# Attention and two expert layers on one core: dividing by the softmax row sums after the product with the values instead of before it

## The chip, the cores and the metric

The kernel runs on 1 core of one Trainium2 chip. The metric is the device time of one execution in microseconds (us), the median of several executions. The engines are named as in the profile: PE (TensorE matmul), PEld (TensorE weight load), DVE (VectorE), ACT (ScalarE), POOL (GpSimd) and SP (SyncE, which here issues every DMA).

## The reference

```python
scores = scale * np.matmul(q, k.transpose(0, 1, 3, 2))
...
scores = np.where(causal, -1000000000.0, scores + np.minimum(bias, 0.0))
scores = scores - np.max(scores, axis=-1, keepdims=True)
attn = np.exp(scores)
attn = attn / (np.sum(attn, axis=-1, keepdims=True) + 1e-09)
return np.matmul(attn, v).astype(np.float32)
...
x = np.ascontiguousarray(attn_out.transpose(0, 2, 1, 3)).reshape(B * S, H * D)
a = x @ w_a
b = x @ w_b
return (a * b @ w_out).astype(np.float32)
...
h = x @ w_in
r = np.maximum(h, 0.0)
g = r * r
return (g @ w_out).astype(np.float32)
```

There are 4 batches of 8 heads, 576 positions and a head dimension of 64; `bias` comes from a running sum of `s`. The attention's output, 2304 tokens of 512 numbers, goes through a gated layer (512 to 1536 and back) and then through a second layer (512 to 2048 and back). Everything is 32-bit.

## The kernel before

**Order of the work.** One function records all operations into a `Plan` (L73 to L246) and the plan then decides, by a table of costs and by ranks (L77), on which of its allowed engines each operation runs and in what order each engine's queue stands. An operation may list several engines: `on_dve`, `on_act`, `on_gps` (L324 to L330). Each queue is then executed in that fixed order. All engine instructions are issued at L246, so the profile's rows all say L246 and are told apart by tile names. Every DMA is issued by SP, in one queue.

**Stages.** Attention of batch 0 is recorded first (stream "first", L936). Then come the twelve steps of the first token chunk of the gated layer, each with the decoding of its weights (`split_w`, L805: rearranging 64-bit words into 32-bit numbers, on DVE, ACT and POOL), and in between, the attention of batch 1 (stream "next"). The attention of batches 2 and 3 is recorded beside further chunks of the gated layer (L950 to L953), and the rest of that layer and the second layer follow. A chunk of the gated layer needs the attention output of its tokens from all four pairs of heads: the first chunk needs 512 positions of batch 0.

**Attention of one head.** `softmax` (L554) makes scores in four PSUM banks (tiles `st`, L461), adds the mask and takes the row maximum on DVE (`neg`), and lets ACT write the exponentials into `e` and their row sums into `sum`. Then one DVE reduction adds the partial sums of all five blocks of queries, one DVE instruction takes the reciprocal (both `one`, L626 and L630), and the five blocks of `e`, 64 to 576 columns wide, 1600 columns in all, are multiplied by it in place, each on DVE, ACT or POOL as the plan likes (L631 to L642). `weigh` (L645) transposes pieces of `e` on PE (`pt`), copies them to SBUF (`ph`), and multiplies them with the values (`av`); its transposes read the "w" parts of `e`, which the multiplications write. The result, 64 rows a head, is copied to `u` (two heads of a pair fill its 128 partitions). In batches 2 and 3 the operands are split in a high and a low part, and `u` is the sum of two halves of `av`.

**Where `u` goes.** `attention` (L711) rounds `u` of batch 0 to a high and a low part (`x0`, both read by the first chunk's matmuls `ab`) and writes its last 64 columns to DRAM (`xd`); for the other batches all of `u` goes to `xd`, from where later chunks load it.

Of the kernel before, what the change touches and what calls it, by code (L numbers as in the profile page):

```python
# [7 lines left out]
F32 = mybir.dt.float32  # L8
# [8 lines left out]
P = 128  # L17
# [231 lines left out]
def attention_moe_moe(tc, q, k, v, s, w_a, w_b, w_out, w_in2, w_out2, out):  # L249
# [55 lines left out]
    def scratch(shape, dtype, name):  # L305
        return pl.fixed(lambda: pools["dram"].tile(shape, dtype, name=name))
# [63 lines left out]
    wlo = [scratch([HD, P, 2, GRP, P], F32, f"wlo{g}") for g in range(NG)]  # L370
    cd = scratch([B * H, 2, S], F32, "cd")


# [76 lines left out]
    for i in range(4):  # L450
        t = [at_const([P, *n], F32, f"{z}{i}") for z, n in (("neg", [NJ + 2]), ("sum", [NJ, 3]), ("one", [NJ]))]
        for x in t[::2]:
            gps("memset", NJ + 2, x, 1.0)

        for c, x in ((0, 1.0), (1, 0.0), (2, 1e-9)):
            gps("memset", NJ, t[1][:, :, c : c + 1], x)
        small.append(t)
# [95 lines left out]

    def softmax(b, p, h, head):  # L554

        nq = len(kb)
        nm = f"{b}_{p}_{h}"
        hh = 2 * p + h
        neg, tot, one = small[count[1] % 4]
        count[1] += 1  # L560
        place = {}
        held = []
        for i, pieces in enumerate(banks):
# [60 lines left out]
            held = []  # L624
        qs = slice(0, nq)
        dve(  # L626
            "tensor_reduce", 3 * nq, out=one[:, qs], in_=tot[:, qs], op=ALU.add, axis=AX.X,
            reads=[tot.part(c) for c in range(nq + 1)],
        )
        dve("reciprocal", nq * 6, one[:, qs], one[:, qs])  # L630
        for blk, (e, off) in place.items():  # L631
            at_, m = kb[blk]
            n = at_ + m
            ee, r = e[:m, off : off + n], one[:m, blk : blk + 1]
            parts = [(blk, 0)] if n <= 512 else [(blk, 0), (blk, 288)]
            kw = {"reads": [e.part(x) for x in parts]}
            ways = [on_dve("tensor_scalar", n, ee.part((blk, "w")), ee, r, None, op0=ALU.mult, each=0.52)]
            ways.append(on_act("mul", n, ee.part((blk, "w")), ee, r))
            ways.append(
                on_gps("tensor_tensor", n, out=ee.part((blk, "w")), in0=ee, in1=r.to_broadcast([m, n]), op=ALU.mult)  # L640
            )
            pl.call(*ways)  # L642
        return place

    def weigh(b, p, h, head, place, chunk, u):  # L645
# [4 lines left out]
        for i, keys in enumerate(key_banks):  # L650
            ps = bank(f"pt{nm}_{i}", "t")
            calls, ins, off, spans = [], [ident], 0, []
            for j in keys:
                k0, m = kb[j]
                c0 = max(k0, g0)
                for blk in range(j, len(kb)):
                    at_, mq = kb[blk]
                    if g0 <= at_ < g0 + n:
                        e, eo = place[blk]
                        ins.append(e.part((blk, "w")))  # L660
                        col = off + at_ - c0
                        calls.append(
                            ("transpose", (ps[:m, col : col + mq], e[:mq, eo + k0 : eo + k0 + m], ident[:mq, :mq]), {})
                        )
                w = g0 + n - c0
                spans.append((j, m, c0 - g0, w, off))
                off += w
# [36 lines left out]


    first = [[at([P, FIRST], F32R, "x0", 2 * ND, f"x0{z}_{d}") for d in range(ND)] for z in range(2)]

# [3 lines left out]
    def attention(b):  # L711
        steps = []

        def unit(p):
# [5 lines left out]
            def one(h):  # L720
                def f():
                    if h == 0:
                        st["u"] = at([P, S], F32, "u", 1, f"u{b}_{p}")
                    place = softmax(b, p, h, st["h"][h])
                    for chunk in weight_banks:
                        weigh(b, p, h, st["h"][h], place, chunk, st["u"])
                    if h == 1:
                        u = st["u"]
                        if b == 0:
                            xh, xl = first_x(p, 0, FIRST)  # L730
# [464 lines left out]
```

## Time and profile before

| | |
|---|---|
| median of 3 runs | 1093.37 us (1091.91 to 1094.2) |
| profiled execution, its own time | 1088.79 us |
| its span, first to last instruction | 1087.0 us |
| PE busy | 1054.8 us (97%), 5376 matmuls |
| PEld busy | 920.4 us (85%) |
| DVE busy | 707.7 us (65%) |
| ACT busy | 502.2 us (46%) |
| POOL busy | 307.6 us (28%) |

The profile is of one execution. An engine's busy time is the union of its instructions; matmuls overlap in it, so a busy PE need not be at its peak. The row of PE in 40 slices of the span reads `5998999999999999999999999999999999999998` and that of DVE `5877899988877888736747445676546434652432`: the first quarter of the span and the rest differ.

### The profile page before, as it was taken

The page shows a single profiled execution, that of the slowest core. Times are in us where ns is not written, and L with a number is a line of the kernel's source. Part 1 is how long each engine was busy: PE and PEld are TensorE (multiplying, and loading weights), DVE is VectorE, ACT ScalarE, POOL GpSimd, SP SyncE. Part 2 cuts the span into 40 slices and gives each one's busy share as a digit, 9 for nine tenths or more (in the row PEclk, how much of TensorE's full clock was granted, in tenths as well). Part 3 has the DMA queues.
Part 4 walks back from the last instruction along what each step waited for, and adds up shares of the span by engine and source line. Part 5 has one row for each costly group of instructions (what it writes and reads, how often), then busy time and mean ns, then how long its engine had stood idle before and what let it go on. Part 6 is the DMA issues. An engine that isn't in the chain of part 4 may idle for free.

```text
span 1087.0 us, 15586 instructions
## 1 busy us (share of the span) xinstructions
PE 1054.8 (97%) x5376; PEld 920.4 (85%) x5376; DVE 707.7 (65%) x1494; ACT 502.2 (46%) x1169; POOL 307.6 (28%) x263
## 2 busy tenths in 40 slices
PE   5998999999999999999999999999999999999998
PEld 3655777777899998999999999998988899889887
DVE  5877899988877888736747445676546434652432
ACT  4665777666667556624333123354423222332222
POOL 2535657565333324105224202323202000200000
PEclk9988999999999999999999999999999999999999
DMA  6543576756544446248879777364535333343311
GB/s 201 173 131 114 177 216 211 230 167 191 160 151 141 141 136 191 85 134 287 293 253 313 258 265 250 142 253 172 192 144 187 146 123 136 112 163 122 136 69 58
DMA packets 94063, 190.84 MB, mean 176 GB/s; under 512 B 10256, under 2 KB 56336, under 8 KB 93984
## 3 DMA queue, kind: packets, MB, share of 16 engines
q1 hardware_dynamic: 93984, 189.85, 51.8%
q8 instruction: 42, 0.69, 0.3%
q14 instruction: 37, 0.30, 0.1%
HBM read 143.58 MB, written 37.37 MB: 166 GB/s over the span
## 4 chain that ended last, share of the span: by engine, by line
PE 86%; DVE 8%; DMA 3%; issue 1%; ACT 1%; SPq 1%; POOL 0%; ACTq 0%; DVEq 0%; POOLq 0%
PE ab L246 24%; PE po L246 18%; PE py L246 11%; PE pa L246 9%; PE av L246 6%; PE st L246 5%; PE pt L246 5%; PE pc L246 5%; PE pb L246 2%; DVE e L246 1%; DVE roomxl L246 1%; DVE st L246 1%; SPq L246 1%; DMA roomxl<-in_moe_w_out 1%; DMA raw_2q<-in_q 1%
## 5 line engine op out<-in xcount | busy, mean ns | idle before, releaser
L246 PE MATMUL ab<-x,wh 128*128 128x512 f32 (+1 forms) x384 | 117.0, 386 | 0.0
L246 ACT ACTIVATE e<-st,neg 128x192 f32<-128x192 f32 (+2 forms) x192 | 91.2, 479 | 38.4 <-DVE neg L246 33.5
L246 PE MATMUL ab<-xh,wh 128*128 128x448 f32 x288 | 106.2, 369 | 0.0
L246 PE MATMUL ab<-xl,wh 128*128 128x448 f32 x288 | 105.3, 366 | 0.0
L246 PE MATMUL ab<-xh,lo 128*128 128x448 f32 x288 | 105.2, 365 | 0.0
L246 ACT COPY s<-pa 128x384 f32<-128x384 f32 x72 | 34.4, 481 | 137.8 <-PE pa L246 137.7
L246 PE MATMUL pt<-ident,e 128*128 128x128 f32 (+2 forms) x480 | 83.8, 284 | 12.4 <-DVE e L246 7.7
L246 PE MATMUL py<-gh,wh 128*128 128x448 f32 (+1 forms) x240 | 90.7, 378 | 0.0
L246 PE MATMUL po<-w2o,gxh 128*128 128x512 f32 x288 | 89.3, 391 | 0.0
L246 PE MATMUL po<-w2o,gh 128*128 128x512 f32 x288 | 89.2, 391 | 0.0
L246 PE MATMUL py<-gh,loo 128*128 128x448 f32 (+1 forms) x240 | 89.0, 371 | 0.0
L246 PE MATMUL py<-gl,wh 128*128 128x448 f32 (+1 forms) x240 | 88.9, 371 | 0.0
L246 PEld LDWEIGHTS pt<-ident,e 128*128 128x128 f32 (+2 forms) x480 | 54.2, 135 | 37.8 <-issue 10.7
L246 DVE TENSOR_TENSOR ab<-ab,a 128x448 f32<-128x448 f32 (+1 forms) x60 | 38.6, 643 | 67.6 <-PE ab L246 64.0
L246 PEld LDWEIGHTS ab<-x,wh 128*128 128x128 f32 x384 | 71.7, 190 | 9.5
L246 PE MATMUL av<-ph,val 128*128 128x256 f32 (+3 forms) x256 | 78.3, 397 | 1.4 <-DVE u L246 0.7
L246 DVE CUSTOM_DVE_ANT_0 st<-st,mask 64x64 f32<-64x64 f32 (+4 forms) x160 | 68.2, 434 | 13.8 <-PE st L246 8.6
L246 ACT CAST gh<-ab 128x448 fp32r<-128x448 f32 (+1 forms) x60 | 32.6, 543 | 85.0 <-DVE ab L246 84.9
L246 DVE TENSOR_TENSOR v<-pc,s 128x384 f32<-128x384 f32 x48 | 26.6, 554 | 68.3 <-ACT s L246 67.2
L246 PEld LDWEIGHTS po<-w2o,gh 128*128 128x128 f32 x288 | 53.5, 188 | 9.2
L246 ACT COPY a<-ab 128x448 f32<-128x448 f32 (+1 forms) x60 | 32.5, 542 | 62.2 <-PE ab L246 61.8
L246 PEld LDWEIGHTS po<-w2o,gxh 128*128 128x128 f32 x288 | 53.4, 188 | 8.6
(247 smaller groups left out, 2733.5 us busy)
## 6 DMA issues: line engine op xcount, KB each, us to landing
w<-w2q SPq DMA_DIRECT2D x48, 896.0 KB
lo<-wlab SPq DMA_DIRECT2D x48, 512.0 KB
loo<-wlo SPq DMA_DIRECT2D x40, 384.0 KB
w2r<-in_moe_w_in SPq DMA_DIRECT2D x16, 512.0 KB
w2or<-in_moe_w_out SPq DMA_DIRECT2D x16, 512.0 KB
w2q<-w2h SPq DMA_DIRECT2D x8, 896.0 KB
w2q<-w2l SPq DMA_DIRECT2D x8, 896.0 KB
roomxh<-in_moe_w_a SPq DMA_DIRECT2D x10, 512.0 KB
```

The costliest lines, as they stand in the source:

```text
L246: getattr(eng, method)(*map(real, args), **{k: real(a) for k, a in kw.items()})
```

## The change

The multiplication of the 1600 columns of `e` by the reciprocal sums is gone, and the transposes read the exponentials as ACT leaves them. In its place the result `u` of a pair of heads, 576 columns, is multiplied. There the row sums belong to columns, so they have to be turned round and spread over 64 partitions each: in batch 0 by spreading them to 128 columns (`wide`, on ACT or DVE) and transposing five pieces on PE into PSUM (`rs`), from which DVE multiplies; in the other batches by one small transpose, a copy (`rows`), a DMA to DRAM (`rd`) and two DMAs that read it back once for each of 64 partitions (`wide`), after which POOL or DVE multiplies. `u` and the reciprocals get two buffers.

```diff
-    def softmax(b, p, h, head):
+    def softmax(b, p, h, head, one):
...
-        qs = slice(0, nq)
+        qs = one[:, h * nq : h * nq + nq].part(h)
         dve(
-            "tensor_reduce", 3 * nq, out=one[:, qs], in_=tot[:, qs], op=ALU.add, axis=AX.X,
+            "tensor_reduce", 3 * nq, out=qs, in_=tot[:, :nq], op=ALU.add, axis=AX.X,
             reads=[tot.part(c) for c in range(nq + 1)],
         )
-        dve("reciprocal", nq * 6, one[:, qs], one[:, qs])
-        for blk, (e, off) in place.items():
...
-            pl.call(*ways)
+        dve("reciprocal", nq * 6, qs, qs)
         return place
...
-                        ins.append(e.part((blk, "w")))
+                        ins += [e.part((blk, x)) for x in ((0,) if at_ + mq <= 512 else (0, 288))]
...
+    def divide_far(b, p, one, u):
+
+        nq = len(kb)
+        ps = bank(f"rs{b}_{p}", "t")
+        pe(107, [("transpose", (ps[: 2 * nq, :P], one, ident), {})], ps, [one.part(0), one.part(1), ident])
+        rows = at([P, P], F32, "rows", 2, f"rows{b}_{p}")[: 2 * nq]
+        copy(P, rows, ps[: 2 * nq, :P], psum=True)
+        far = rd[b, p]
+        dma(far, rows, 2)
+        wide = at([P, nq * P], F32, "wide", 2, f"wide{b}_{p}")
+        for h in range(2):
+            dma(
+                wide[h * D : h * D + D].part(h),
+                far[h * nq : h * nq + nq].rearrange("(o j) q -> o (j q)", o=1).to_broadcast([D, nq * P]), 164,
+            )
+        for o, n, w in ((0, 64, 0), (64, S - 64, P)):
+            kw = {"out": u[:, o : o + n].part("r"), "in0": u[:, o : o + n].part("r"), "in1": wide[:, w : w + n], "op": ALU.mult}
+            pl.call(
+                on_gps("tensor_tensor", n, **kw), on_dve("tensor_tensor", n, two=True, **kw),
+                reads=[u.part((a, g)) for a in (0, 64) for g, _, _ in weight_banks],
+            )
+
+    def divide(b, p, one, u):
+
+        nq = len(kb)
+        if b:
+            return divide_far(b, p, one, u)
+        wide = at([P, nq * P], F32, "wide", 2, f"wide{b}_{p}")
+        copy(
+            nq * P, wide.rearrange("p (j h d) -> p j h d", j=nq, h=2),
+            one.rearrange("p (h j o) -> p j h o", j=nq, o=1).to_broadcast([P, nq, 2, D]),
+        )
+        for g0, n, key_banks in weight_banks:
+            ps = bank(f"rs{b}_{p}_{g0}", "t")
+            calls = []
+            for j, (at_, m) in enumerate(kb):
+                if g0 <= at_ < g0 + n:
+                    r = wide[:m, j * P : j * P + P]
+                    calls.append(("transpose", (ps[:, at_ - g0 : at_ - g0 + m], r, ident[:m, :m]), {}))
+            pe(len(calls) * 107, calls, ps, [wide, ident])
+            dve(
+                "tensor_tensor", n, out=u[:, g0 : g0 + n].part((0, g0)), in0=u[:, g0 : g0 + n].part((0, g0)),
+                in1=ps[:, :n], op=ALU.mult, reads=[u.part((64, g0))],
+            )
...
-                        st["u"] = at([P, S], F32, "u", 1, f"u{b}_{p}")
-                    place = softmax(b, p, h, st["h"][h])
+                        st["u"] = at([P, S], F32, "u", 2, f"u{b}_{p}")
+                        st["one"] = at([P, 2 * len(kb)], F32, "one", 2, f"one{b}_{p}")
+                    place = softmax(b, p, h, st["h"][h], st["one"])
...
+                        divide(b, p, st["one"], u)
```

The plan makes a new order out of this. Three places of it follow; in the names the first digits are batch, pair and head, the last number only counts tiles.

**First head, PE.** Before, the first transposes `pt` of the exponentials of head 0 stand behind the last scores `st` of both heads:

```order
L246 MATMUL st0_0_1_1_171<-fk1_81,fq1_89 128x448
L246 MATMUL st0_0_1_1_171<-fk1_81,fq1_89 64x64
L246 MATMUL st0_0_0_2_178<-fk0_77,fq0_79 128x288
L246 MATMUL st0_0_1_2_185<-fk1_81,fq1_89 128x288
L246 MATMUL st0_0_0_3_190<-fk0_77,fq0_79 128x288
L246 MATMUL st0_0_1_3_200<-fk1_81,fq1_89 128x288
L246 MATMUL pt0_0_0_0_0_236<-ident_73,e0_0_0_1_176 64x64
L246 MATMUL pt0_0_0_0_0_236<-ident_73,e0_0_0_0_164 64x128 x2
L246 MATMUL pt0_0_0_0_1_241<-ident_73,e0_0_0_0_164 128x128 x3
```

Now:

```order
L246 MATMUL st0_0_1_1_163<-fk1_81,fq1_89 128x448
L246 MATMUL st0_0_1_1_163<-fk1_81,fq1_89 64x64
L246 MATMUL st0_0_0_2_170<-fk0_77,fq0_79 128x288
L246 MATMUL pt0_0_0_0_0_177<-ident_73,e0_0_0_1_168 64x64
L246 MATMUL pt0_0_0_0_0_177<-ident_73,e0_0_0_0_157 64x128 x2
L246 MATMUL pt0_0_0_0_1_181<-ident_73,e0_0_0_0_157 128x128 x3
L246 MATMUL st0_0_1_2_188<-fk1_81,fq1_89 128x288
L246 MATMUL st0_0_0_3_194<-fk0_77,fq0_79 128x288
L246 MATMUL av0_0_0_0_199<-ph0_0_0_0_0_186,val0_0_96 128x320
L246 MATMUL av0_0_0_0_199<-ph0_0_0_0_1_190,val0_0_96 128x256
L246 MATMUL st0_0_1_3_209<-fk1_81,fq1_89 128x288
```

The first two groups of transposes have moved ahead of three of the last score matmuls.

**End of batch 0, PE.** `ab` are the first matmuls of the gated layer. Before, scores and transposes of batch 1 stand ahead of the first of them:

```order
L246 MATMUL st1_0_1_0_1016<-t2k1_0_1_879,t2q1_0_1_871 128x320
L246 MATMUL st1_0_1_0_1016<-T11_912 128x192
L246 MATMUL st1_0_1_0_1016<-t2k1_0_1_879,t2q1_0_1_871 128x192
L246 MATMUL st1_0_1_1_1026<-T11_912 128x448
L246 MATMUL st1_0_1_1_1026<-t2k1_0_1_879,t2q1_0_1_871 128x448
L246 MATMUL st1_0_1_1_1026<-T11_912 64x64
L246 MATMUL st1_0_1_1_1026<-t2k1_0_1_879,t2q1_0_1_871 64x64
L246 MATMUL pt1_0_0_0_0_1049<-ident_73,e1_0_0_1_972 64x64
L246 MATMUL pt1_0_0_0_0_1049<-ident_73,e1_0_0_0_949 64x128 x2
L246 MATMUL pt1_0_0_0_1_1055<-ident_73,e1_0_0_0_949 128x128 x3
L246 MATMUL ab0_0_0_1063<-x00_0_424,wh0_0_273 128x512
L246 MATMUL ab0_0_0_1063<-x01_0_431,wh0_0_273 128x512
```

Now:

```order
L246 MATMUL av0_3_1_320_904<-ph0_3_1_320_0_891,val0_3_572 128x256 x2
L246 MATMUL rs0_3_0_909<-ident_73,wide0_3_867 128x64
L246 MATMUL rs0_3_0_909<-ident_73,wide0_3_867 128x128 x2
L246 MATMUL av0_3_1_320_904<-ph0_3_1_320_1_902,val0_3_572 128x256
L246 MATMUL rs0_3_320_921<-ident_73,wide0_3_867 128x128 x2
L246 MATMUL av0_3_1_320_904<-ph0_3_1_320_1_902,val0_3_572 128x128
L246 MATMUL av0_3_1_320_904<-ph0_3_1_320_2_913,val0_3_572 128x256
L246 MATMUL ab0_0_0_958<-x00_0_394,wh0_0_288 128x512
L246 MATMUL ab0_0_0_958<-x01_0_404,wh0_0_288 128x512
```

The transposes `rs` stand between the last products with the values, and `ab` follows directly on them; the 20 score matmuls and 6 transposes of batch 1 that stood ahead of the first `ab` come behind its group of 12.

**SP, a pair of batch 1.** Before, `u` goes to DRAM in one step, between loads of weights (`roomxh`, `roomxl`) and values:

```order
L246 DMA roomxl_152<-in_moe_w_out 128x1024
L246 DMA wlo1_1215<-wl4_2_1390 256x1x128 x2
L246 DMA val1_2_1435<-in_v 64x128
L246 DMA xd1_1448<-u1_0_1118 128x576
L246 DMA roomxh_130<-in_moe_w_b 128x4x256
L246 DMA val1_2_1435<-in_v 128x4x128
L246 DMA wlab5_1477<-wl5_1416 128x1024
```

Now, of the same pair:

```order
L246 DMA wlo1_1159<-wl4_2_1350 256x1x128 x2
L246 DMA rd1_0_1397<-rows1_0_1384 10x128
L246 DMA roomxh_129<-in_moe_w_b 128x4x256
L246 DMA wide1_0_1420<-rd1_0_1397 64x640 x2
L246 DMA val1_2_1448<-in_v 64x128
L246 DMA val1_2_1448<-in_v 128x4x128
```

The small `rd` and the two `wide` that read it back are new, with one weight load between them; `xd` follows 9 rows below the second `wide`. Each of the 12 pairs of batches 1 to 3 has such a group.

## Rows read from the trace of the kernel before

**Rows 1.** Stages: us, then busy (instructions) by engine, PEclk, DMA share, GB/s.

```profile
21.00:111.00 90.00, 77.42 (x344) 52.57 (x345) 72.75 (x209) 58.24 (x164) 41.48 (x33) 0.92 0.46 145
111.00:280.00 169.00, 163.55 (x830) 130.32 (x828) 150.19 (x326) 116.33 (x289) 104.02 (x78) 0.99 0.62 194
280.00:480.00 200.00, 199.58 (x1192) 183.10 (x1191) 154.62 (x400) 119.22 (x321) 55.32 (x49) 1.00 0.45 140
480.00:1087.00 607.00, 602.23 (x2993) 547.65 (x2991) 320.06 (x532) 200.62 (x376) 103.53 (x75) 1.00 0.52 186
```

**Rows 2.** The chain that ended last, by line: 21 to 111, then 111 to 280 us.

```profile
by line: PE av L246 31.5%; PE st L246 18.9%; PE pt L246 16.7%; DVE e L246 7.3%; issue 5.4%; DMA fq<-in_q 3.1%; DVE st L246 2.5%; DVE u L246 2.1%; DVE roomxl L246 1.9%; DVE x L246 1.7%; POOL t2k L246 1.7%; ACT ph L246 1.4%; DVE roomxh L246 1
...
by line: PE ab L246 18.8%; PE av L246 9.1%; PE pt L246 7.5%; DVE roomxl L246 6.5%; issue 4.5%; DMA roomxl<-in_moe_w_out 4.4%; DMA raw_2q<-in_q 4.3%; DVE e L246 3.7%; PE py L246 3.6%; DMA roomxh<-in_moe_w_b 3.5%; PE st L246 3.4%; DVE st L246
```

**Rows 3.** Timeline, first head: start, us, instruction, [idle before <- releaser].

```profile
13.26 0.62 ACT L246 ACTIVATE e<-st,neg 128x448 f32<-128x448 f32 x1
...
22.04 2.00 DVE L246 TENSOR_SCALAR e<-e,one 64x64 f32<-64x64 f32 x3
...
23.36 1.79 PE L246 MATMUL pt<-ident,e 64*64 64x64 f32 x6 [3.44 <-DVE e L246]
```

**Rows 4.** Groups: the divisions in 21 to 111, then 111 to 280 us.

```profile
L246 DVE TENSOR_SCALAR e<-e,one 64x64 f32<-64x64 f32 (+4 forms) x23 | 13.9, 639 | 0.1
L246 ACT ACTIVATE e<-e,one 128x192 f32<-128x192 f32 (+4 forms) x17 | 9.1, 577 | 2.8 <-DVE neg L246 1.4 <-DVE one L246 1.3
L246 POOL TENSOR_TENSOR e<-e,one 128x320 f32<-128x320 f32 (+2 forms) x5 | 3.9, 779 | 7.6 <-DVE one L246 7.6
...
L246 DVE TENSOR_SCALAR e<-e,one 128x320 f32<-128x320 f32 (+4 forms) x20 | 12.8, 668 | 0.1
L246 ACT ACTIVATE e<-e,one 128x192 f32<-128x192 f32 (+4 forms) x23 | 11.2, 532 | 1.9 <-DVE one L246 1.8
L246 POOL TENSOR_TENSOR e<-e,one 128x576 f32<-128x576 f32 (+4 forms) x8 | 7.4, 938 | 7.3 <-DVE one L246 7.3
```

**Rows 5.** Groups and timeline: operations like the added ones.

```profile
L246 DVE TENSOR_TENSOR u<-av,vl 64x320 f32<-64x320 f32 (+1 forms) x4 | 1.8, 453 | 0.1
L246 DVE TENSOR_TENSOR y<-py,y 128x512 f32<-128x512 f32 x8 | 5.5, 685 | 1.1 <-PE py L246 1.0
L246 POOL TENSOR_TENSOR x<-u,x 128x512 fp32r<-128x512 f32 x3 | 3.8, 1277 | 3.7 <-DVE x L246 3.7
...
116.47 0.66 PE L246 MATMUL pt<-ident,e 128*128 128x128 f32 x4
```

**Rows 6.** Clock: the three stretches below full grant, columns as in group 1.

```profile
65.00:75.00 10.00, 9.84 (x35) 6.47 (x36) 6.72 (x25) 5.58 (x16) 0.48 (x1) 0.66 0.67 206
90.00:100.00 10.00, 9.15 (x35) 6.48 (x36) 6.64 (x17) 3.76 (x12) 5.94 (x5) 0.66 0.46 141
110.00:115.00 5.00, 4.46 (x16) 3.60 (x17) 4.94 (x10) 2.82 (x9) 4.14 (x4) 0.66 0.52 147
```

**Rows 7.** Timeline of PE: what it waited for ahead of each.

```profile
65.16 1.13 PE L246 MATMUL st<-fk,fq 65*128 65x320 f32 x4 [2.01 <-ACT fq L246]
...
88.74 0.24 PE L246 MATMUL pt<-ident,e 64*64 64x64 f32 x1 [2.40 <-ACT e L246]
...
110.54 0.92 PE L246 MATMUL pt<-ident,e 64*64 64x64 f32 x6 [2.32 <-DVE e L246]
```

**Rows 8.** Chain: DMA pieces (start, us); SP's own waits (total, times, longest).

```profile
6.25 1.68 DMA fk<-cum
...
153.05 7.36 DMA roomxl<-in_moe_w_out
189.70 5.89 DMA roomxh<-in_moe_w_b
262.89 7.20 DMA raw_2q<-in_q
...
SPq L246 <- PE av L246: 7.4, 2, 6.9
```

More of the change, by code (lines that the diff above doesn't have):

```diff
@@ L371, in attention_moe_moe @@
     cd = scratch([B * H, 2, S], F32, "cd")
+    rd = {(b, p): scratch([2 * ((S + P - 1) // P), P], F32, f"rd{b}_{p}") for b in range(1, B) for p in range(NP)}
     def const(shape, dtype, name):
@@ L450, in attention_moe_moe @@
     for i in range(4):
-        t = [at_const([P, *n], F32, f"{z}{i}") for z, n in (("neg", [NJ + 2]), ("sum", [NJ, 3]), ("one", [NJ]))]
-        for x in t[::2]:
-            gps("memset", NJ + 2, x, 1.0)
+        t = [at_const([P, *n], F32, f"{z}{i}") for z, n in (("neg", [NJ + 2]), ("sum", [NJ, 3]))]
+        gps("memset", NJ + 2, t[0], 1.0)
         for c, x in ((0, 1.0), (1, 0.0), (2, 1e-9)):
@@ L558, in softmax @@
         hh = 2 * p + h
-        neg, tot, one = small[count[1] % 4]
+        neg, tot = small[count[1] % 4]
         count[1] += 1
@@ L624, in softmax @@
             held = []
-        qs = slice(0, nq)
+        qs = one[:, h * nq : h * nq + nq].part(h)
         dve(
-            "tensor_reduce", 3 * nq, out=one[:, qs], in_=tot[:, qs], op=ALU.add, axis=AX.X,
+            "tensor_reduce", 3 * nq, out=qs, in_=tot[:, :nq], op=ALU.add, axis=AX.X,
             reads=[tot.part(c) for c in range(nq + 1)],
         )
-        dve("reciprocal", nq * 6, one[:, qs], one[:, qs])
-        for blk, (e, off) in place.items():
[L632 to L641, printed above, removed]
-            pl.call(*ways)
+        dve("reciprocal", nq * 6, qs, qs)
         return place
```

## Prediction

> **What bounds the kernel now.** I read the stages first. PE is busy for 99 to 100% of the last two, 280 to 480 and 480 to 1087 us, and only 77.4 of 90 us in 21 to 111 and 163.6 of 169 us in 111 to 280 [rows 1]. A busy PE need not be at its peak, so I compare its weight loads too: they fill 90% of the last stage (547.65 of 607 us) and 92% of the third, but 58% of the first (52.57 of 90) and 77% of the second (130.32 of 169). At the last stage's 90% the weight loads of the first would fit in 58.3 us and those of the second in 144.5 us. So there is room of some 32 + 24 us in the first two stages, and hardly any behind them: 607 us of second-half matmuls stay as they are whatever attention does. In the first two stages the fullest other engine is DVE, with 72.75 of 90 us and 150.19 of 169 us [rows 1]. The gain of the change has to come from there.
>
> The Trainium skill, Perfetto Trace Analysis, section Identifying the Most-Contended Engine, says the same of the choice between the two measures: occupancy of matmuls flatters PE, and the busy share of LDWEIGHTS is to be used. By matmul occupancy the room would be 12.6 + 5.4 = 18.0 us instead of 56; the second stage's term below would then be cut from 7 to 5.4 us and the predicted time would be 1080.3.
>
> Next the chain of waits. In the first stage it runs through the divisions (DVE `e`) for 7.3% of 90 us = 6.6 us, in the second for 3.7% of 169 us = 6.3 us [rows 2]. Where this comes from is plain in the first head: ACT had written the last exponentials of its first banks at 13.26 + 0.62 us, but the transposes that need no more than these start at 23.36 us, right behind the divisions of 22.04 to 24.04, since the row sums are added once for all five blocks [rows 3]. In the second stage the chain has something else: three pieces of 7.36, 5.89 and 7.20 us in which it waits for loads of weights and of q [rows 8].
>
> **What goes.** All 160 divisions. In the first stage these are 13.9 us on DVE, 9.1 on ACT and 3.9 on POOL, in the second 12.8, 11.2 and 7.4 [rows 4]. The reduction and the reciprocal stay, but nothing of the transposes waits for them any more.
>
> **What comes, first stage (batch 0).** Eight DVE multiplications out of PSUM, 320 or 256 columns on 128 partitions. The nearest row is the addition `u` from `av`, of the same widths and also out of PSUM: 453 ns, 3.6 us in all. The upper bound is the addition of 512 columns, 685 ns, 5.5 us [rows 5]. Four ACT copies of 640 columns cost somewhat more than its divisions' mean of 577 ns [rows 4], perhaps 3 us in all, against 9.1 that go: hidden. The 20 transposes `rs` at 0.66 / 4 = 0.165 us [rows 5] are 3.3 us of PE; its 12.6 idle us cover them, and if that idle time should vanish they cost what they take.
>
> DVE is left with 13.9 - 3.6 = 10.3 us less. What of this shortens the stage? At the low end only what the chain shows, 6.6 us. At the high end all of it, and the rest of the stage in proportion to DVE's 81%: 12.7 us. I take **9 us**, near the DVE figure, since the earlier transposes also fill PE while DVE still reduces scores.
>
> Against that stands a new wait at the end of the stage. Between the last product of pair 3 and the first `ab` there are now two DVE multiplications, about 0.9 us by the same row, and their handovers, and the scores of batch 1 that PE had in hand are queued behind `ab`. Only a hold of well under 1 us if DVE comes at once; up to 4 us if it stands behind weight decoding of the other tiles. I take **+2 us**. The moved scores themselves change where the stages part, not their sum.
>
> **What comes, second stage (batch 1).** Four pairs are multiplied by the spread sums, in 512 and 64 columns, mostly on POOL: 1.28 us for 512 columns [rows 5], under 6 us for four pairs, against 7.4 us of divisions that POOL loses [rows 4]. DVE takes over one of the wide ones, 0.7 us, and some copies of 128 columns, so that it is relieved of about 11 us. The low bound for the stage is that the loads already on its chain, 20 us together, hold it: nothing gained. The middle is the chain's share of the divisions, 6.3 us; the high end is 11 us over DVE's 89%, 12.4 us. I take **7 us**, near the chain's share, since loads do not get shorter.
>
> **Third stage (batches 2 and 3).** PE has no room there, so the removed divisions save nothing, and 8 small transposes at no more than 0.165 us cost **+1.3 us**. The rest of their path (copy, DRAM and back, 12 pairs in the whole kernel) ends at `xd`, which the token chunks read only much later: nothing, as long as no queue stops. What is queued behind it on SP is a rival below.
>
> **Clock.** In three stretches the granted clock means 0.66, a mixture of 2.4 and 1.2 GHz: 25 us in all, in which 8.5 us of full-rate clock are missing [rows 6]. Each followed a stop of PE by 2.0 to 2.4 us: one for a scaled q, two for `e` [rows 7]. The two behind `e` should not come in this form, which could give back up to 3.4 + 1.7 us; but PE will still have pauses in a stage that DVE limits, and the new one at its end. Between nothing and 5.1, I take **2 us**.
>
> **The sum.** -9 + 2 - 7 + 1.3 - 2 = -14.7 us against the profiled execution, 1088.8 to 1074.1. That execution is 4.6 us under the median of the runs shown, 1093.37; taken from the median, the prediction is **1078.7 us**.
>
> **Rivals.**
>
> *DVE holds both stages alone.* Then both high ends hold, 12.7 + 12.4, the end costs 0.5, and 5 us of clock come back: 1093.4 - 12.7 + 0.5 - 12.4 + 1.3 - 5 = 1065.1. For it speaks that DVE is the fullest engine beside PE in both stages and that ACT and POOL get free time to take over copies; against it the loads on the second stage's chain [rows 8]. Chance 0.18.
>
> *The loads hold the second stage.* Decoding goes on at the pace at which weights arrive, and only the chain's share of the first stage is won: 1093.4 - 6.6 + 2 + 1.3 = 1090.1, a little lower or higher as the end of batch 0 goes. For it speaks that the 20 us of loads in the chain are more than its divisions there. Against: a buffer of raw weights is freed by DVE and POOL work, so lighter engines ask for the next load earlier. Chance 0.15; in a third of it the difference is within 0.2%. That the change does not do what it says (transposes still waiting for sums) is excluded for the first head by the new order, and what is left of that is in this case.
>
> *SP stops (slower).* SP issues in order. For each pair it waits for `rows`, behind a PE transpose and a copy, issues `rd`, and must see it land before the first `wide`. The landing of a small transfer took 1.68 us after its issue [rows 8]; a wait of SP for PE's `av` reached 6.9 us [rows 8]. Both together are 8.6 us a pair, 34 us for the four pairs of the second stage, in which no weight load starts. As long as loads issued earlier are still running, this costs nothing. It decides from about 4.2 us a pair that reach the chain: four times that takes the whole gain of 14.7 us and 2.2 more. At 6.9 us a pair, 27.6 us in all and the second stage's 7 us gone as well, the time is 1078.7 + 7 + 27.6 = 1113. For it: the chain there already stops for loads, and the new order has one load or none between `rd` and `wide`. Against: DMA engines are busy for 62% of that stage [rows 1], so loads are mostly under way. Chance 0.12.
>
> **Chances.** The forecast, 1070 to 1087, gets 0.55. A measurement of this kernel can tell about 0.2%, 2.2 us, from no change. Faster by more: 0.55 + 0.18 + 0.08 of the loads' case = 0.81; within: 0.05 of that case and 0.01 of SP's; slower: 0.02 of the loads' case and 0.11 of SP's. The range goes from 1064, which takes in DVE alone but for its far half, to 1092, which takes in the loads' case but for its worst: some 0.2 are left out, most of it SP's. The forecast's own range is 1070 to 1087.
>
> **What would show it.** Right: the first `ab` comes before 104 us (9 us of gain less 2, and the scores moved behind it), the first transposes of head 0 begin before 18 us, DVE's busy time falls by about 22 us up to the end of batch 1, and the last stage keeps its 607 us. Wrong: the stretch between 111 and 280 us keeps its length with SP rows that wait for `rows` or `rd` on the chain; a stop of PE over 4 us ahead of `ab` with the clock at half behind it; or third-stage idle time at `rs`.

## The result and the profile after

The changed kernel takes 1079.8 us, the median of 4 runs (1078.28 to 1080.99); the kernel before beside it 1093.66 us (4 runs, 1091.91 to 1094.2). The ratio is 0.9883, 95% interval 0.9861 to 0.9905. In a second set of runs the changed kernel took 1082.84 us (12 runs, 1078.81 to 1089.28), with a ratio of 0.9931 (0.9908 to 0.9954). So the gain is real, and by the medians it is 13.9 us in the first set and 8.3 us in the second, larger one. Each set of runs below has executions of the kernel before beside it, and its ratio is to those. The forecast of 1078.7 us was met, but not by the terms that it was made of.

The busy times of the whole profiled execution (span 1077.8 us); DVE's has fallen by 22.9 us:

```profile
PE 1053.0 (98%) x5408; PEld 919.6 (85%) x5408; DVE 684.8 (64%) x1449; ACT 477.5 (44%) x1117; POOL 284.9 (26%) x244
```

The stages of the changed kernel, with the columns of [rows 1] and, below the first two rows, its stretches; the first row is the first stage without its end, the second its end:

```profile
15.00:92.00 77.00, 75.01 (x351) 49.62 (x350) 60.37 (x177) 47.42 (x140) 20.17 (x15) 1.00 0.43 140
92.00:104.00 12.00, 8.02 (x27) 5.85 (x27) 10.07 (x16) 5.75 (x12) 7.90 (x5) 0.72 0.58 164
...
21.00:111.00 90.00, 84.03 (x397) 57.75 (x396) 73.95 (x198) 56.23 (x156) 29.88 (x22) 0.96 0.46 141
111.00:280.00 169.00, 163.17 (x861) 131.11 (x860) 143.51 (x335) 112.68 (x289) 104.38 (x81) 1.00 0.71 217
280.00:480.00 200.00, 199.67 (x1181) 184.24 (x1179) 152.29 (x384) 108.78 (x291) 61.02 (x54) 1.00 0.53 165
480.00:1077.80 597.80, 593.00 (x2947) 539.13 (x2946) 305.81 (x512) 192.43 (x362) 86.52 (x62) 1.00 0.51 181
```

In the 90 us from 21 us on PE does 397 matmuls where it did 344. In the stretch 111 to 280 us it is busy for 163.17 us, where it was for 163.55 [rows 1].

In the timeline of PE, the first head's transposes come 6.5 us earlier than at 23.36 us [rows 3] and wait for nothing:

```profile
11.73 5.24 PE L246 MATMUL st<-fk,fq 65*128 65x320 f32 x10
16.90 1.52 PE L246 MATMUL pt<-ident,e 64*64 64x64 f32 x6
```

At the end of batch 0 the timelines of DVE and then of PE show how the new multiplications stand ahead of the first token chunk (start, duration, instruction, in brackets the idle time before it and what ended it):

```profile
90.80 0.49 DVE L246 TENSOR_TENSOR u<-u,rs 128x320 f32<-128x320 f32 x1 [0.95 <-PE rs L246]
...
92.63 0.42 DVE L246 TENSOR_TENSOR u<-u,rs 128x256 f32<-128x256 f32 x1 [0.74 <-ACT u L246]
...
93.31 0.42 DVE L246 CAST x<-u 128x512 fp32r<-128x512 f32 x1
...
98.17 1.72 DVE L246 TENSOR_TENSOR t2q<-raw_0q,T 64x576 fp32r<-64x576 f32 x1
```

```profile
92.12 0.72 PE L246 MATMUL ab<-x,wh 128*128 128x512 f32 x2
...
96.55 0.56 PE L246 MATMUL ab<-x,wh 128*128 128x512 f32 x1 [1.85 <-POOL x L246]
...
99.95 0.64 PE L246 MATMUL st<-t2k,t2q 128*128 128x320 f32 x1 [2.14 <-DVE t2q L246]
```

PE starts `ab` at 92.12 us with the operands of pairs 0 to 2. For pair 3's it waits 1.85 us, and then 2.14 us for the scaled q of batch 1. The clock falls there, as it did in [rows 6]; between 104 and 290 us its mean is 1.00:

```profile
96.00:102.00 6.00, 3.31 (x11) 2.49 (x12) 4.78 (x7) 1.55 (x3) 4.75 (x4) 0.57 0.57 143
```

The eight multiplications out of PSUM and the 20 transposes of the sums, by tile (min/median/max in ns, first and last start); a multiplication, 449 ns, costs what its nearest row said [rows 5]:

```profile
L246 PE MATMUL rs<-ident,wide x20: 271/272/328, 35.0 to 91.1; 128*128 128x128 f32 x16, 64*128 64x64 f32 x4
L246 DVE TENSOR_TENSOR u<-u,rs x8: 416/449/489, 35.6 to 92.6; 128x320 f32<-128x320 f32 x4, 128x256 f32<-128x256 f32 x4
```

The chain of waits in 111 to 280 us has lost the divisions' 3.7% [rows 2], and has other things in their place:

```profile
by line: PE py L246 16.1%; DVE roomxl L246 9.6%; PE ab L246 9.0%; PE av L246 8.6%; DMA roomxh<-in_moe_w_a 7.6%; PE pt L246 5.1%; PE st L246 5.0%; issue 4.4%; DMA raw_1q<-in_q 3.7%; DMA xl<-xd 3.6%; DVE ph L246 3.2%; DVE roomxh L246 2.8%; DV
```

**A ledger for the stages.** The planner orders the work anew in every kernel, so a stretch of time doesn't hold the same work twice. For the comparison each matmul is given the time to the start of the next one that a fifth of its kind (same tiles, same shape) stay under in the trace before, and these times, in us, are added up in the order in which PE does them; the added transposes `rs` count as nothing. The table says at which us of the span so much work was done, from one profiled execution of each kernel (each label is an experiment below; before and after are there twice):

```
work                 50     60    100    200    300    450    600    end
before             96.4  112.0  158.4  277.2  383.3  539.3  690.3  1087.0
before, again      98.9  114.5  160.8  283.2  389.3  545.4  696.4  1093.8
after              83.8  103.6  150.2  268.2  375.8  530.9  682.1  1077.8
after, again       84.0  103.8  151.0  271.4  379.1  534.1  685.3  1081.0
e1 batch 0 only    84.3  104.2  150.2  266.7  373.6  540.2  691.2  1087.4
e2 batches 1-3     98.7  112.9  161.8  274.4  382.3  537.9  688.9  1085.2
e3 wait kept       88.0  105.4  153.8  267.2  373.4  531.6  682.6  1079.0
e4 work kept       84.0  101.0  148.6  273.5  382.6  539.2  690.2  1086.3
e7 not divided     83.8  103.7  151.0  265.0  372.7  527.4  678.4  1074.5
e8 PE throughout   84.6  104.4  153.0  274.3  384.3  542.5  693.6  1088.3
e9 before, loads   96.3  112.0  158.4  274.1  380.2  536.3  687.3  1084.0
e10 after, loads   84.7  104.5  151.1  264.6  373.3  528.2  679.4  1075.7
e11 pair 3 on DVE  84.2  102.0  152.7  271.7  378.3  534.0  685.0  1080.7
e12 and TURN 2     84.3  101.1  146.9  267.9  377.1  533.0  687.2  1084.2
```

In both pairs of before and after 12.6 to 14.9 us are won by work 50, some 4 us of them given back by work 60, and from there to the end nearly nothing changes: -8.4 and -10.7 at work 60, -7.5 and -10.2 at work 300. Counted in other ways (the median in place of the fifth, say) single rows move by some 1 to 2 us, so smaller differences between different plans are not read here. Part of the early gain is clock: by work 50 the two profiles of the kernel before lack 6.2 and 8.0 us of full-rate clock (0.83 is granted on the mean from 60 to 96.4 us in the first; 0.74 up to 80 and 0.85 up to 98.9 us in the second), and those of the changed kernel lack none.

### The profile page after: what moved, and what is told of

The parts are those of the page before. It is cut to its first block, busy times and chain, and to the rows that moved or that the text cites. A ratio compares the mean times of both kernels' runs of the same rounds, so it can differ in the third digit from the quotient of the medians.

```text
span 1077.8 us, 15538 instructions
## 1 busy us (share of the span) xinstructions
PE 1053.0 (98%) x5408; PEld 919.6 (85%) x5408; DVE 684.8 (64%) x1449; ACT 477.5 (44%) x1117; POOL 284.9 (26%) x244
## 4 chain that ended last, share of the span: by engine, by line
PE 88%; DVE 6%; DMA 3%; issue 1%; ACT 1%; SPq 1%; POOL 0%; POOLq 0%; ACTq 0%; DVEq 0%
PE ab L246 24%; PE po L246 18%; PE py L246 14%; PE pa L246 9%; PE av L246 6%; PE st L246 6%; PE pc L246 5%; PE pt L246 4%; PE pb L246 2%; DVE roomxl L246 2%; DMA roomxh<-in_moe_w_a 1%; SPq L246 1%; DMA raw_1q<-in_q 1%; DMA xl<-xd 1%; DVE ph L246 1%
## 5 line engine op out<-in xcount | busy, mean ns | idle before, releaser
L246 PE MATMUL pt<-ident,e 128*128 128x128 f32 (+2 forms) x480 | 80.3, 278 | 2.9 <-ACT ph L246 1.7
L246 PEld LDWEIGHTS ab<-x,wh 128*128 128x128 f32 x384 | 71.5, 190 | 12.5 <-POOL x L246 2.3
L246 DVE CUSTOM_DVE_ANT_0 st<-st,mask 128x192 f32<-128x192 f32 (+4 forms) x160 | 67.5, 437 | 17.2 <-PE st L246 14.1
L246 PE MATMUL av<-ph,val 128*128 128x256 f32 (+3 forms) x256 | 75.3, 382 | 1.9 <-DVE u L246 1.6
L246 PEld LDWEIGHTS pt<-ident,e 128*128 128x128 f32 (+2 forms) x480 | 52.0, 132 | 21.5 <-issue 6.4
```

Source lines behind the costliest of these rows:

```text
L246: getattr(eng, method)(*map(real, args), **{k: real(a) for k, a in kw.items()})
```

## The experiments

**Batch 0 alone, batches 1 to 3 alone.** A set `OLD` of batches that keep the old division:

```diff
+    OLD = (1, 2, 3)                  # e1;  e2: (0,)
...
+        if b in OLD:
+            for blk, (e, off) in place.items():
+                ...                  # the old multiplication of e
-                        ins += [e.part((blk, x)) for x in ((0,) if at_ + mq <= 512 else (0, 288))]
+                        ins += [e.part((blk, x)) for x in (("w",) if b in OLD else (0,) if at_ + mq <= 512 else (0, 288))]
...
-                        divide(b, p, st["one"], u)
+                        if b not in OLD:
+                            divide(b, p, st["one"], u)
```

> The division is moved in batch 0 alone; batches 1 to 3 divide their exponentials as before (u and the reciprocals keep two buffers). Both stages theory (first stage 9 less 2 and clock 2, second stage 7): about 9 us of the 14 us are won, 1084 to 1086 us. First stage alone theory: the whole gain, 1079 to 1082 us. New order by chance theory (any new plan of this kernel differs by several us): no relation, anything between 1075 and 1100 us.

> The division is moved in batches 1 to 3 alone; batch 0 divides its exponentials as before. Both stages theory: 7 us less 1.3 us are won, 1087 to 1089 us, with the first matmul of the gated layer at about 111 us as before. First stage alone theory: within 2 us of the kernel before, 1092 to 1096 us, or slower by the DRAM round trip. The two parts' gains should add up to about 14 us if they are independent.

Batch 0 alone: 1089.66 us, ratio 0.9994 (0.9967 to 1.0022), nothing. Batches 1 to 3 alone: 1086.11 us, ratio 0.9952 (0.9931 to 0.9973), some 5 us, which the theory of the first stage alone excludes. The two do not add up to the whole's 8 to 14 us. Only the theory that any new plan differs by several us leaves room for batch 0 alone coming to nothing. The ledger shows that it has the whole of the early gain (373.6 at work 300, against 375.8 after) and loses it between 300 and 450. There the waits of PE in 480 to 560 us, and the stretches, are

```profile
500.00:525.00 25.00, 20.02 (x93) 17.57 (x92) 20.39 (x34) 13.69 (x24) 8.77 (x8) 0.96 0.81 264
525.00:550.00 25.00, 25.00 (x114) 22.93 (x114) 10.80 (x19) 6.47 (x14) 3.34 (x3) 0.90 0.79 274
...
PE ab L246 <- DVE x L246: 5.0, 1, 5.0
```

PE stops for 5.0 us for the `x` of the next token chunk and then runs at a lower clock; the changed kernel's trace has no wait of PE in 480 to 560 us at all. By the timelines, attention's last matmul comes at 486.6 us in e1 and at 446.9 us in the changed kernel, and the chunk that follows needs that attention's output. But the late end alone does not make the stop: in the two profiles of the kernel before attention's last matmul comes at 478.2 and 484.3 us, and neither has a wait of PE in 480 to 560 us. So beside the changed kernel e1 loses its gain two stages behind batch 0, in this stop and the clock that falls with it; what makes the stop in e1's order is open.

**The wait kept, the work kept.** In e3 the transposes wait for the reciprocals again, with no division of `e`. In e4 they don't wait, but the 160 multiplications are done, into a spare tile that nobody reads:

```diff
-        calls, ins, off, spans = [], [ident], 0, []
+        calls, ins, off, spans = [], [ident, one.part(h)], 0, []        # e3
```

```diff
         dve("reciprocal", nq * 6, qs, qs)
+        for blk, (e, off) in place.items():                             # e4
+            dump = at([P, S], F32, "dump", 2, ...)[:m, :n]
+            ...                      # dump = e * r on DVE, ACT or POOL
```

> The changed kernel, but every transpose of exponentials also waits for its head's reciprocal sums, as it did when it waited for the division; the divisions stay gone. Engine load theory (DVE, ACT and POOL time is what was won): most of the gain stays, 1081 to 1085 us. Early transposes theory (the wait was what cost): most of it goes, 1088 to 1093 us.

> The changed kernel, but the 160 multiplications of the exponentials are still done, into a spare tile that nothing reads, on whichever of DVE, ACT and POOL the plan picks; no transpose waits for them. Engine load theory: nearly all of the gain goes, 1090 to 1096 us. Early transposes theory: most of it stays, 1080 to 1085 us.

e3: 1084.76 us, ratio 0.9937 (0.9916 to 0.9959). e4: 1087.13 us, ratio 0.9963 (0.9945 to 0.9982). In the timelines of PE the first transposes come at 19.92 us in e3 and at 17.08 us in e4:

```profile
19.92 1.52 PE L246 MATMUL pt<-ident,e 64*64 64x64 f32 x6
```

```profile
17.08 1.52 PE L246 MATMUL pt<-ident,e 64*64 64x64 f32 x6
```

By the ledger e4 has the whole early gain (84.0 at work 50) although its engines do the divisions' work in the first stage again. In e3, at 88.0, 8.4 of the 12.6 us are won. So the work as such, spread as e4 spreads it, is worth next to nothing in the first stage; what is won is a chain from the exponentials to the transposes: 8.4 us for the link of the divisions, with the 6.2 us of missing clock in it (e3's mean grant up to 88 us is 1.00), and 4.2 for that of the sums and reciprocals. By tile in 15 to 92 us, e4's multiplications were spread like this. POOL took the most of them and DVE only ten, 7.8 us where [rows 4] has 13.9, so what the full load on DVE would cost here is not tested:

```profile
L246 POOL TENSOR_TENSOR dump<-e,one x16: 285/506/1522, 26.3 to 87.9; 128x192 f32<-128x192 f32 x6, 64x64 f32<-64x64 f32 x5, 128x448 f32<-128x448 f32 x4, 128x576 f32<-128x576 f32 x1
L246 ACT ACTIVATE dump<-e,one x14: 347/562/771, 26.2 to 88.9; 128x320 f32<-128x320 f32 x5, 64x64 f32<-64x64 f32 x3, 128x448 f32<-128x448 f32 x3, 128x576 f32<-128x576 f32 x2
L246 DVE TENSOR_SCALAR dump<-e,one x10: 376/741/1325, 27.5 to 87.0; 128x576 f32<-128x576 f32 x5, 128x320 f32<-128x320 f32 x3, 128x448 f32<-128x448 f32 x1, 128x192 f32<-128x192 f32 x1
```

Between work 100 and 200 e4 takes 124.9 us (148.6 to 273.5), 6.9 more than the first profile of the changed kernel and 4.5 more than the second: there the work is felt, and by work 300 e4 stands where the kernel before does (382.6 and 383.3). e3, on the other hand, has made good its 4 us by work 200, and in time, ratio 0.9937, it cannot be told from the changed kernel's larger set, 0.9931. So by the ends e3 came out as the theory of engine load said, and e4 between the two theories; the early transposes account for the first stage only.

**Both kernels once more.** The changed kernel unaltered, in five rounds, and one execution of the kernel before:

> The changed kernel again, beside the kernel before, with more executions of both, so that the parts can be set against the whole on one footing. Both theories: 12 to 15 us under the kernel before, ratio 0.986 to 0.989.

> The kernel before, profiled once more: the first profiled execution was 4.6 us under its median. Expected at 1089 to 1094 us. If it is slower than the first profile, the extra time should lie ahead of 530 us; the last stage (480 us to the end in the first profile, 607 us) should be the same within 1 us.

1082.84 us (12 runs) for the changed kernel, 8.3 us and not 12 to 15 under the 1091.14 us (23 runs) of the kernel before, and 1095.6 us for the one execution of the kernel before, 1.6 above what was expected; of its 6.8 us of longer span 6.1 lie ahead of work 450, as expected. The executions of each differ by several us, and the two profiles of each let us see in what: the mean granted clock, and the span, of before and before again, then of after and after again:

```profile
core 0: 1087.0 us, clock 0.992
```

```profile
core 0: 1093.8 us, clock 0.987
```

```profile
core 0: 1077.8 us, clock 0.996
```

```profile
core 0: 1081.0 us, clock 0.994
```

Span times (1 - clock) is the full-rate time that is missing: 8.7 and 14.2 us before, 4.3 and 6.5 us after (to half a us, as the clock is given to 0.001). Without it the spans are 1078.3 and 1079.6 us, and 1073.5 and 1074.5 us. So most of what the two profiles of one kernel differ by is clock, and so is a part of the gain: of the 9.2 and 12.8 us between the pairs, 4.4 and 7.7 are missing clock and some 5 are anything else. The 23 and 12 executions of this set say the same: on the mean 10.5 us are missing before and 5.3 after, and the mean spans without it are 1079.1 and 1076.1 us, so that clock is some 5 of 8 us. It is not all that executions differ by: without it those of the changed kernel still lie between 1072.0 and 1079.7 us. (A clock that falls while PE waits costs less than it is counted at, so the clock's part is an upper bound.)

**The path by DRAM.** In e7 batches 1 to 3 are not divided at all (this part of the computation is left out); in e8 they are divided as batch 0 is, by PE transposes and with no DMA:

```diff
-                        divide(b, p, st["one"], u)
+                        if b == 0: divide(b, p, st["one"], u)           # e7
```

```diff
-        if b: return divide_far(b, p, one, u)                           # e8
```

> Batches 1 to 3 are not divided at all (their 12 transposes, 36 DMAs and 24 multiplications are left out); batch 0 is divided as in the changed kernel. Theory that the DRAM round trip is hidden: within 3 us of the changed kernel, by at most 1.3 us of PE and a little DVE and POOL time, 1076 to 1080 us. Theory that SP's waits for it hold the weight loads of batch 1: 8 us or more faster, under 1072 us.

> Batches 1 to 3 are divided as batch 0 is, by five transposes a pair on PE, without the DRAM round trip: 48 more transposes on PE and 24 multiplications out of PSUM on DVE, 36 DMAs fewer. Theory that the round trip is hidden: slower than the changed kernel by the PE time of the transposes in the PE-bound stretch, 32 to 48 times 0.12 to 0.165 us, 4 to 8 us, and by DVE time: 1083 to 1090 us. Theory that SP's waits cost: faster than the changed kernel.

e7: 1077.86 us, ratio 0.989 (0.9852 to 0.9928); e8: 1089.54 us, ratio 0.9984 (0.9963 to 1.0006). All that stands between `u` and `xd` in three batches costs some 5 us (1082.84 to 1077.86), and by PE it would cost 6.7 us more. The ledger has those 5 us in the second stage: from work 100 to 300 e7 takes 221.7 us, the changed kernel 225.6 and 228.1. A stop of SP of the size of the rival's, 28 us, is excluded by this; a small one is not. In 111 to 290 us of the changed kernel SP waits for `rows` for 4.8 us and for `rd` to land for 5.5 us in all, not the 34 us of the rival.

**Loads of a quarter.** What the second stage's missing gain went to was open. In e9 (from the kernel before) and e10 (from the changed one) the weight loads from the thirteenth on carry a quarter of their bytes, and the rest is decoded from what lies in the buffer; every engine's instructions stand in the same order as in the kernel that each comes from:

```diff
-        dma(raw.rearrange("p (d c) -> p d c", d=ND), src, ...
+        dma(raw.rearrange("p (d c) -> p d c", d=ND)[:, : ND // part], src[:, : ND // part], ...
```

> The kernel before, in which every weight load of the first half from the thirteenth on (all that the stage 111 to 280 us waits for) carries a quarter of its bytes; the tiles are decoded as ever from what lies in the buffer, so the output is not the reference's. The order of the instructions on every engine is unchanged. If the loads hold the second stage: it becomes shorter by most of the 13.25 us of weight loads that its chain shows, so the end comes 6 to 13 us earlier, 1079 to 1085. If DVE or PE hold it (my forecast's view): within 3 us of the kernel before.

> The same quarter loads in the changed kernel, order of the instructions unchanged. If the loads hid what the removed divisions are worth in the second stage: the equal-work difference between this and the kernel before with quarter loads grows from about -9 us at the beginning of the second stage to -14 to -16 at its end, and the time is 1064 to 1073. If the divisions are worth nothing there for another reason (they lie beside PE work whatever the loads do): the difference stays near -9 through the stage, and the two times differ by 8 to 12 us.

e9: 1087.02 us, ratio 0.9954 (0.9932 to 0.9977). e10: 1079.85 us, ratio 0.9882 (0.9851 to 0.9913). The stretch from work 100 to work 300, columns as above, in the kernel before, in e9, in the changed kernel and in e10, and then in e3 and e7:

```profile
158.40:383.30 224.90, 219.81 (x1221) 187.53 (x1219) 190.13 (x460) 147.64 (x384) 105.04 (x84) 1.00 0.56 174
```

```profile
158.40:380.20 221.80, 219.19 (x1221) 187.35 (x1219) 190.63 (x461) 147.43 (x384) 105.63 (x84) 1.00 0.50 150
```

```profile
150.20:375.80 225.60, 221.05 (x1263) 189.82 (x1262) 188.74 (x475) 144.63 (x390) 110.48 (x91) 1.00 0.62 191
```

```profile
151.10:373.30 222.20, 220.34 (x1264) 189.85 (x1262) 187.75 (x474) 144.44 (x390) 111.12 (x91) 1.00 0.56 168
```

```profile
153.80:373.40 219.60, 218.65 (x1221) 187.25 (x1220) 175.17 (x439) 130.23 (x349) 91.21 (x73) 1.00 0.60 184
```

```profile
151.00:372.70 221.70, 219.69 (x1242) 188.70 (x1241) 186.22 (x467) 139.80 (x381) 87.91 (x68) 1.00 0.60 183
```

PE's idle time falls from 5.09 to 2.61 us before and from 4.55 to 1.86 us after; the ledger has -3.1 and -2.5 us at work 300. Between the two kernels with quarter loads lie 6.9 us at work 300, against 7.5 and 10.2 with full loads. So the loads cost both kernels the same 3 us or so, and did not hide what the divisions were worth. By the medians e9 lies 5.5 us under the kernel before of its set (1092.54), between what its two theories expected, and e10 7.2 us under e9, nearer to the 8 to 12 of the second.

What became of the divisions is seen in the first and third line. At equal work DVE is busy for 190.13 us before and 188.74 after: hardly any relief. The plan has put attention of later batches in the place; the mask additions of DVE in the two stretches are

```profile
L246 DVE CUSTOM_DVE_ANT_0 st<-st,mask 128x320 f32<-128x320 f32 (+4 forms) x74 | 31.4, 434 | 1.8 <-PE av L246 0.6 <-PE st L246 0.2
```

```profile
L246 DVE CUSTOM_DVE_ANT_0 st<-st,mask 128x192 f32<-128x192 f32 (+4 forms) x84 | 35.1, 438 | 2.9 <-ACT y L246 1.7 <-PE st L246 0.7
```

and attention's last matmul comes at 446.9 us where it came at 478.2. In the kernel before, PE waits in that stretch for these (total, times, longest):

```profile
PE st L246 <- ACT e L246: 2.1, 2, 1.2
PE pt L246 <- DVE ph L246: 1.1, 1, 1.1
PE pt L246 <- DVE e L246: 0.6, 2, 0.4
PE pt L246 <- DVE pl L246: 0.5, 1, 0.5
PE av L246 <- DVE ph L246: 0.4, 1, 0.4
PE pt L246 <- POOL e L246: 0.2, 1, 0.2
```

Only 0.8 us of it, `e` of DVE and POOL ahead of `pt`, are waits for a division; scores `st` wait for exponentials that still read their bank, the others for copies. That the removal could win nothing here is not shown, though: e3 has the divisions gone too and takes 219.60 us, 5.3 less than the kernel before, with PE idle for 0.95 us; e7 takes 221.70, and e4, which has them back, 234.0. Their plans are in another order (e3's stretch has 74 mask additions), which no run kept fixed, so why e3 gains here and the changed kernel doesn't is open.

**A better end of batch 0.** e11 subtracts pair 3's low part on DVE alone; e12 also moves `TURN` from 4 to 2, so that batch 1's steps are recorded earlier:

```diff
-                            subtract(FIRST, xl, u[:, :FIRST], xh.bitcast(F32))
+                            subtract(FIRST, xl, u[:, :FIRST], xh.bitcast(F32), by="D" if p == NP - 1 else "PD")
...
-    TURN = 4
+    TURN = 2                         # e12
```

> The changed kernel, but the low part of the last pair of batch 0 is subtracted on DVE and never on POOL, whose 1.85 us wait stands ahead of the second group of ab at 96.55 us. If that wait is worth its length: 1 to 3 us less than the changed kernel beside it in the stretch 92 to 104 us (4 us are given back there), and 1 to 2 us at the end, 1078 to 1082. If DVE is the scarcer engine there: the wait of the scaled q (2.14 us) grows by the 0.6 us of the subtraction, and nothing is won.

> As the last one, and in addition the plan takes up batch 1's steps two weight tiles earlier (TURN 2 instead of 4), so that its q, k and scores are ready when batch 0 ends and attention as a whole ends earlier. If the stop at the end of batch 0 is a matter of what PE has in hand: the second wait (2.14 us for the scaled q) goes too, and the time falls by 2 to 4 us against the changed kernel. If the decoding of the weights then comes later: ab waits for wh or wl instead, and the time is the same or up to 5 us more.

e11: 1082.62 us (6 runs), ratio 0.9905 (0.9888 to 0.9922), the changed kernel's time. e12: 1085.52 us, ratio 0.9921 (0.9899 to 0.9943), no better. In PE's timeline of e12 the two waits of 1.85 and 2.14 us become

```profile
96.66 0.50 PE L246 MATMUL ab<-x,wh 128*128 128x512 f32 x1 [1.28 <-DVE x L246]
...
98.10 0.39 PE L246 MATMUL st<-t2k,t2q 128*128 128x320 f32 x1 [0.55 <-DVE t2q L246]
```

and the ledger stands 2.5 us ahead of the changed kernel at work 60 and 3.3 us at work 100. By work 300 the lead is gone (377.1 against 375.8). In e11 1.6 us at work 60 have become 2.5 us behind at work 100. So the stop at the end of batch 0 can be shortened, but what is won there isn't kept. Where e12 loses it was not taken apart. e11 also shows what a new plan does by itself: one subtraction bound to DVE, and attention's last matmul comes at 457.0 us instead of 446.9.

## Why the prediction was right, and where it was wrong

**The time was right, the sum was not.** 1079.8 and 1082.84 us lie close to 1078.7. The terms were -9, +2, -7, +1.3 and -2, -14.7 in all; the profiles have -9.2 and -12.8. With the missing clock counted by itself, the two pairs of profiles give -6.4 and -6.9 by work 50 (first stage), +1.7 and +2.6 by work 60 (end of batch 0), +2.3 and +1.0 from there to work 300 (second stage), -2.4 and -1.8 behind it, and -4.4 and -7.7 of clock. That the time came out is luck in two ways: the clock gave some of what the second stage did not, and the forecast started from 1093.37 us, the median of 3 executions, where 28, 23 and 12 later ones have medians of 1091.12, 1091.14 and 1092.54. In the larger set the gain is 8.3 us.

- **First stage, -9, and the end of batch 0, +2.** Right in kind, and near in size: -6.4 to -6.9 us by work 50 without the clock, some 2 us given back by work 60. The first `ab` came at 92.12 us, the first transposes at 16.90, both well inside the bounds that were set. The forecast put the gain near what DVE loses in work; e4, as far as its spread goes, shows that this work is worth nothing there, and e3 that two links of the wait make up the whole. The chain's 6.6 us for `e` [rows 2], the low end, come near the whole without the clock. At the end of the batch the wait was 1.85 us for `x`, about as forecast; the second one, 2.14 us for a scaled q behind weight decoding on DVE, was not foreseen. Together they come close to the 4 us that were set as a sign of being wrong, and the clock did fall there.
- **Second stage, -7.** This is the step that failed. It came out as +0.9 and +0.5 us (-8.4 to -7.5, -10.7 to -10.2). The room of 24 us was read from PE's weight loads, 77% there against 90% in the last stage [rows 1]. But PE's own row stood at 97%, and behind it were only some 5 us of idle time, half of which went with the loads in e9 and 0.8 us of which were waits for divisions. The chain's 3.7% of divisions [rows 2] were not time that the changed kernel won: other links took their place, as they did for the loads, whose two pieces of weights there, 13.25 us [rows 8], were worth 3 us when cut to a quarter. Nor was DVE relieved by the forecast's 11 us: at equal work it was 1.4, since the plan filled the place with scores of later batches, and the sign that DVE's busy time would fall by 22 us up to the end of batch 1 was missed (12.5 by work 200, 230.3 to 217.8). With the new path left out e7 won 3.2 us on the kernel before in that stretch, and e3, with the path, 5.3: some of the term can be had in another order, but not in the one that the plan made. The Trainium skill (Perfetto Trace Analysis, Identifying the Most-Contended Engine) judges headroom by the weight loads' share and the share of peak arithmetic, not by matmul occupancy; the measurement of this stage went with the matmul row.
- **The rival of the loads** foresaw that the second stage would give nothing, but not why: e9 and e10 refute its mechanism. The rival of DVE alone falls with the second stage; the rival of SP's stop, at its size, falls with e7.
- **Third stage, +1.3.** Not seen: work 300 to 450 took 156.0 us before and 155.1 after. The matmul behind a small transpose starts 0.03 us after it where 0.165 was taken, which would make 0.2 us for eight:

```profile
284.21 0.27 PE L246 MATMUL rs<-ident,one 128*10 128x128 f32 x1
284.24 0.37 PE L246 MATMUL av<-ph,vs 128*128 128x256 f32 x1
```

- **Clock, -2.** The stretches that [rows 6] show, 65 to 75 and 110 to 115 us, run at full clock now; a new one at 96 to 102 us does not. Over the whole span 4.4 and 7.7 us less clock is missing in the two pairs of profiles, 5.2 on the mean of the larger set, where the forecast took 2 out of at most 5.1. This was the term sized too small.
- **Last stage.** It kept its time: from the first matmul of the second layer (`pa`) to the end 387.4 us before and after. But e1 shows that what stands ahead of that point is not simply a fixed sum of matmuls: between work 300 and 450 it takes 166.6 us, 11.5 more than the changed kernel, 5.0 of them a stop for a late `x`. The forecast's sentence that the last stage stays as it is whatever attention does held for this change, and not for half of it.

## What to carry to other kernels

A link of the chain of waits gives the place where to look, and not the price: loads of 13 us were worth 3, and 6 us of divisions nothing in the plan that was made; cut the suspect itself to a quarter, with the order of the work kept, to learn its price. In this stage, whose matmul row was at 97%, no kernel here won much more than the 5 us of idle time left in that row, however few the weight loads. Compare stages by equal work and not by equal time when a planner reorders everything, set the missing clock apart, and take a profile of each kernel twice before a few us are assigned to a cause. A planner may spend the time of a removed operation on other work, which a comparison of busy times by equal work shows.

## What was not expected of the hardware

Executions of one program differ in part by falls of the clock. The same place in the two profiles of the changed kernel, PE's timeline, first of one and then of the other:

```profile
186.52 0.55 PE L246 MATMUL pt<-ident,e 128*128 128x128 f32 x3 [0.63 <-ACT ph L246]
187.00 0.70 PE L246 MATMUL av<-ph,val 64*128 64x256 f32 x2
187.62 0.50 PE L246 MATMUL py<-gh,wh 128*128 128x512 f32 x1
187.96 0.39 PE L246 MATMUL py<-gl,wh 128*128 128x512 f32 x1
188.19 0.39 PE L246 MATMUL py<-gh,loo 128*128 128x512 f32 x1
```

```profile
187.52 0.90 PE L246 MATMUL pt<-ident,e 128*128 128x128 f32 x3 [0.88 <-ACT ph L246]
188.35 1.22 PE L246 MATMUL av<-ph,val 64*128 64x256 f32 x2
189.50 0.79 PE L246 MATMUL py<-gh,wh 128*128 128x512 f32 x1
190.09 0.63 PE L246 MATMUL py<-gl,wh 128*128 128x512 f32 x1
190.52 0.63 PE L246 MATMUL py<-gh,loo 128*128 128x512 f32 x1
```

Ahead of both, PE had stopped by 0.7 us some 2.5 us earlier. After a wait of 0.63 us the 512-column matmuls follow each other in 0.23 us, at 2.4 GHz; after one of 0.88 us in 0.43 us, at 1.2 GHz, and the mean granted clock of the 5 us from 190 on is 1.00 in the one and 0.58 in the other. A wait that is longer by a quarter of a us is so followed by some 3 us of span, about what the two profiles differ by (in the ledger 0.8 us at work 100 and 3.2 us at work 200); that the longer wait is what makes the clock fall is not shown. This is one reason why a gain of a few us could be seen here only over many executions.
